# Which parts of g are turned by DMA is chosen per unit, and the table of leads is refitted, in a fused attention and mixture-of-experts kernel

## The chip, the cores and the metric

The kernel runs on one core of a Trainium2 chip, in one launch. Its time is the device time in microseconds, and a kernel's figure is the median of several runs. The core has a matrix engine (PE, with weight loads shown apart as PEld), a vector engine (DVE), an activation engine (ACT), a general engine (POOL) and a queue engine (SP) that issues most DMAs; a few are issued by ACT. Each engine works through its own instructions in the order in which they were written into the program, and waits at an instruction until what it needs is there.

## The reference

Three stages follow each other, all in float32, with 2304 = 4 x 576 tokens of 512 = 8 x 64 features. `tau` is 0.02, `E` is 8 experts with 4 slots each.

```python
scores = scale * np.matmul(q, k.transpose(0, 1, 3, 2))          # 4 x 8 heads, 576 x 576, 64 features a head
thresh = np.max(scores, axis=-1, keepdims=True) - tau
scores = np.where(scores >= thresh, scores, -1000000000.0)
attn = np.exp(scores - max); attn = attn / (sum + 1e-09)
x = concat of heads of np.matmul(attn, v)                       # 2304 x 512

g = np.maximum(x @ w_in, 0.0) ** 2                              # w_in 512 x 2048
x = g @ w_out                                                   # w_out 2048 x 512

logits = x @ phi                                                # phi 512 x 32
d = softmax of logits over the tokens
slot_input = d.T @ x                                            # 8 experts x 4 slots x 512
slot_out[e] = np.maximum(slot_input[e] @ w1[e], 0.0) @ w2[e]    # 512 x 1024 and 1024 x 512
out = softmax of logits over the slots @ slot_out
```

## The kernel before

The three stages are fused and overlap. **Attention** runs as 80 score tiles. For each, PE makes the scores (line L708 and its neighbours in the first tiles, in float32; L726 in the others, with float16 halves), DVE finds the maximum (L752), ACT takes the exponential (L764), DVE drops what is under the threshold (L768), ACT and POOL split the result into high and low halves (L787, L791), SP turns the halves by a DMA transpose (L798), and PE multiplies with v (L895, L900). DVE evacuates the result as rows of x.

**The FFN** works in nine units of 256 tokens, as soon as attention has delivered them. In each, x is split into float16 halves (L1214, L1219), and eight pairs of blocks follow, of 24 matmuls each (L1248; `f_a` and `f_b`), after which ACT applies relu (L1258) and the square (L1266). Their result, g, has tokens along its free axis: 16 blocks of 128 features by 256 tokens, in the tiles `gt`.

**What comes after a unit** is written by `post`, while the next unit's first pair runs. PE multiplies g with w_out phi to get logits (L1001, 16 instructions, of which the first 12 need the pairs 0 to 5 and the last 4 the pairs 6 and 7). ACT evacuates them into the tile l (L1079), PE adds up the partial sums (L1008) and transposes them (L1014), DVE updates the running maximum (L1026, L1028), ACT takes the exponential dT (L1032), and PE transposes that (L278 on dT). Then the weighted sum of g over the tokens is needed (L1166, into an accumulator, merged at L1176). For this, g must have its tokens along the partitions, so it is turned, in four parts `j` of a unit, each of two token blocks `t`. Either PE turns a part with 8 transposes of 128x128 (`f_turn`, printed as L278 on gt), and ACT evacuates it (`f_gk`, L1137); or the DMA turns it: ACT copies the part's two gt tiles side by side into a buffer of 16-bit halves (`f_part`, L1107, two instructions), SP issues one DMA transpose (`f_move`, L1112), and DVE puts the halves together again (`f_join`, L1147, four instructions). The buffers of this path are from the `raw64` pool, which the attention's loads use as well. The ninth unit's transposes are always on PE.

**The end.** The experts' weights (w1, w2) and w_out, in pieces of 0.5 or 1 MB, come by SP into buffers as these become free: some when attention's pools end, some (`w8`) as the last unit's L1248 have read w_in, some when the first tail matmuls (L1435) have read theirs. A hand-written tail (L1435 and later) turns the accumulated sums into slot inputs (with w_out), runs the experts (L1462, L1519, L1542, L1562) and writes the output (L1592, L1571).

**What sets the order.** Up to the tail, a planner (`Plan`) runs when the program is built. Each operation is added with an engine, a cost, what it depends on, the buffers that it takes and frees, and a key. At each step an engine takes, of the operations that are ready, that with the lowest key, and its instructions are written in this order. The key is a due time plus a number from the table `LEAD`, one for each kind of operation and each of five parts of the program:

```python
part = state.get("unit", 0) // 2 if abs(key) > FKEY / 2 else sum(key >= c for c in CUTS)
return plan.add(eng, cost, fn, deps, key + LEAD[kind][part], *args, ...)
```

So a changed table moves instructions on all engines, DMA issues among them, and no instruction's own work.

## Time and profile before

| | |
|---|---|
| median of 3 runs | 605.29 us (603.68 to 608.01) |
| the profiled execution | 604.63 us, its span 602.8 us |
| mean granted clock of PE | 0.993 |
| PE busy | 560.2 us (93%), its weight loads 387.7 (64%) |
| ACT busy | 464.8 us (77%) |
| DVE busy | 438.5 us (73%) |
| POOL busy | 290.8 us (48%) |

The profile is of one execution. Its span runs from the first to the last instruction, and the rest of its time lies around that. A busy share is a mean over stretches with different limits, so the rows that follow are mostly of single stretches, and of what an engine waited for there. In the chain that ended last each piece is what held up the next one, back from the last instruction. Matmuls are pipelined, so an instruction's mean duration is longer than its share of the busy time; the cost of one is the group's busy time divided by its count.

### The profile page before, as it was taken

How to read it: one execution, taken by the hardware profiler on the slowest of the kernel's cores; microseconds unless marked ns; L12 is line 12 of the kernel's file. 1: busy time of each engine (PE TensorE's matmuls, PEld its weight loads, DVE VectorE, ACT ScalarE, POOL GpSimd, SP SyncE). 2: the span in 40 equal slices, each digit the busy share in tenths (PEclk: the TensorE clock that was granted, in tenths of full speed). 3: DMA queues.
4: the chain of work that ended last, by engine and by line, in shares of the span. 5: the costliest groups of instructions: out<-in, count | busy, mean ns of one | idle time of the engine just before them, and what ended most of it. 6: DMA issues, size and time to landing. Idle time of an engine off the chain costs nothing.

```text
span 602.8 us, 14200 instructions
## 1 busy us (share of the span) xinstructions
PE 560.2 (93%) x5238; PEld 387.7 (64%) x5238; DVE 438.5 (73%) x1249; ACT 464.8 (77%) x880; POOL 290.8 (48%) x464
## 2 busy tenths in 40 slices
PE   1899998999999999999999999999999999999972
PEld 0556565656776787677677677767778777753331
DVE  3999999899969678888989999896951434232242
ACT  4899999898979897998998998998956776341122
POOL 1345875587857554875776486767620000010000
PEclk9999999899999999999999999999999999999998
DMA  8984574699956676659768767567629998999997
GB/s 266 368 277 132 177 263 147 196 217 211 227 106 135 129 149 154 119 134 171 159 101 167 145 124 115 109 125 132 121 40 301 232 318 201 335 369 360 407 323 261
DMA packets 171348, 120.97 MB, mean 201 GB/s; under 512 B 136592, under 2 KB 152720, under 8 KB 169360
## 3 DMA queue, kind: packets, MB, share of 16 engines
q1 hardware_dynamic: 170704, 117.98, 74.2%
q10 hardware_dynamic: 576, 2.10, 1.1%
q8 instruction: 41, 0.67, 0.5%
q14 instruction: 27, 0.22, 0.1%
HBM read 73.72 MB, written 8.91 MB: 137 GB/s over the span
## 4 chain that ended last, share of the span: by engine, by line
PE 70%; ACT 11%; DVE 9%; DMA 3%; issue 2%; POOL 2%; SPq 1%; DVEq 0%; ACTq 0%; POOLq 0%
PE mm L1248 30%; PE mm L278 8%; PE s L726 7%; PE po L895 5%; ACT raw L343 3%; PE mm L1166 3%; PE mm L1001 3%; ACT e L764 3%; DVE e L768 2%; PE mm L1462 2%; DVE u L752 2%; ACT pt L835 2%; PE mm L1519 2%; DMA w<-in_moe_w_dram 2%; DMA qt<-in_q_dram 1%
## 5 line engine op out<-in xcount | busy, mean ns | idle before, releaser
L1248 PEld LDWEIGHTS <-w 128*128 128x128 f16 x1728 | 166.1, 99 | 30.1 <-issue 11.5
L791 POOL TENSOR_TENSOR hl<-e,hl 128x288 f16<-128x288 f32 x192 | 148.5, 798 | 45.4 <-ACT hl L787 38.6
L1248 PE MATMUL mm<-xh,w 128*128 128x256 f16 x1152 | 149.7, 273 | 0.0
L768 DVE SCALAR_TENSOR_TENSOR e<-u,sm,e 128x576 f32<-128x576 f32 x144 | 122.5, 869 | 14.8 <-ACT e L764 11.1
L764 ACT ACTIVATE e<-u,sm 128x576 f32<-128x576 f32 x144 | 109.1, 772 | 9.4 <-DVE u L752 5.7
L758 POOL TENSOR_SCALAR sm<-sm,tau_p 128x1 f32<-128x1 f32 x144 | 79.3, 556 | 66.9 <-DVE u L752 55.9
L1248 PE MATMUL mm<-xl,w 128*128 128x256 f16 x576 | 86.4, 273 | 0.0
L752 DVE TENSOR_SCALAR_CACHE_REDUCE u<-s,raw 128x576 f32<-128x576 f32 x90 | 71.3, 808 | 7.7 <-PE s L726 7.3
L1258 ACT ACTIVATE gt<-mm,scl 128x512 f32<-128x512 f32 x72 | 49.2, 683 | 34.2 <-PE mm L1248 34.1
L787 ACT ACTIVATE hl<-e 128x576 f16<-128x576 f32 x96 | 63.9, 677 | 2.6 <-DVE e L768 2.1
L1412 POOL MEMSET cv<- 128x512 f32 x4 | 1.9, 527 | 97.8 <-PE mm L1166 97.8
L752 DVE TENSOR_SCALAR_CACHE_REDUCE u<-s,nscale 128x576 f32<-128x576 f32 x54 | 42.8, 809 | 5.7 <-PE s L713 5.4
L343 ACT ACTIVATE raw<-raw 128x512 f16<-128x512 bf16 x32 | 43.1, 1367 | 4.2 <-DMA raw<-in_moe_w_in_dram 4.2
L1266 ACT ACTIVATE gt<-gt 128x512 f32<-128x512 f32 x72 | 45.0, 625 | 1.0
L726 PEld LDWEIGHTS <-qt 128*128 128x128 f16 (+3 forms) x400 | 22.1, 99 | 25.5 <-issue 17.4
L855 POOL TENSOR_SCALAR sm<-sm 128x4 f32<-128x4 f32 (+1 forms) x48 | 20.4, 424 | 35.4 <-DVE e L768 32.3
L895 PE MATMUL po<-pt,vh 128*64 128x256 f16 x576 | 36.0, 275 | 0.0
L726 PE MATMUL s<-kt,qt 128*128 128x512 f16 (+1 forms) x200 | 32.9, 289 | 1.8 <-DVE u L752 1.6
L895 PEld LDWEIGHTS <-vh 128*64 128x64 f16 x576 | 29.6, 110 | 5.6 <-issue 5.4
L835 ACT ACTIVATE pt<-mm 128x512 f32<-128x512 f32 x48 | 28.6, 610 | 5.3 <-PE mm L278 5.1
L1137 ACT ACTIVATE gk<-mm 128x512 f32<-128x512 f32 x50 | 27.1, 595 | 5.8 <-PE mm L278 5.7
L278 PE MATMUL mm<-ident_r,e 128*128 128x128 f32 x192 | 30.0, 286 | 1.3 <-DVE e L768 1.0
(211 smaller groups left out, 987.0 us busy)
## 6 DMA issues: line engine op xcount, KB each, us to landing
w<-in_moe_w_dram SPq DMA_DIRECT2D x15, 1024.0 KB, 9.7
w<-in_moe_w_dram SPq DMA_DIRECT2D x26, 512.0 KB, 8.0
raw<-in_moe_w_in_dram SPq DMA_DIRECT2D x16, 511.8 KB, 7.0
raw<-in_moe_w_out_dram SPq DMA_DIRECT2D x16, 511.8 KB, 4.0
raw<-in_v_dram SPq DMA_DIRECT2D x20, 256.0 KB, 4.0
w_out<-cv SPq DMA_DIRECT2D x16, 256.0 KB, 3.5
w<-w_out SPq DMA_DIRECT2D x8, 512.0 KB, 7.6
kt<-in_k_dram SPq DMA_DIRECT2D x10, 320.0 KB, 4.1
```

What stands on the lines that cost most here:

```text
L278: nc.tensor.transpose(out_, in_, ident[:n, :n])
L343: nc.scalar.activation(x[:, :, 3].bitcast(F16), x[:, :, 2].bitcast(BF16), AF.Copy)
L726: nc.tensor.matmul(o0, d["qh"][r, a, q0], kk, start=full, stop=not full)
L752: nc.vector.tensor_scalar(u, o["s"][:, s0:s0 + S], d.get("nscale", nscale), None, ALU.mult, ALU.min, accum_out=gd["sm"][:, c:c + 1])
L758: nc.gpsimd.tensor_scalar(sm[:, 4 + c:5 + c], sm[:, c:c + 1], tau_p, None, ALU.add)
L764: nc.scalar.activation(e, o["u", a], AF.Exp, scale=-1.0, bias=gd["sm"][:, c:c + 1])
L768: nc.vector.scalar_tensor_tensor(e, o["u", a], sm[:, 4 + c:5 + c], e, ALU.is_le, ALU.mult, accum_out=sm[:, 8 + c:9 + c])
L787: nc.scalar.activation(o["hl"][:, a * S:(a + 1) * S], o["e"][:, a * S:(a + 1) * S], AF.Copy)
L791: nc.gpsimd.tensor_tensor(o["hl"][:, 2 * S:][:, i], o["e"][:, i], o["hl"][:, i], ALU.subtract)
L895: nc.tensor.matmul(po[64 * a:64 * a + 64, :n_], d["vh"][:, y, c0:c0 + D], gd["pt"][:, :, c + 5 * a + m, :], start=i == 0 and m == 0, stop= ...
L1248: nc.tensor.matmul(o["h"][:, i * NU:(i + 1) * NU], a, c, start=n_ == 0, stop=n_ == len(terms) - 1)
L1258: nc.scalar.activation(g, o["h"], AF.Relu, scale=down)
```

## The change

The tuple `DTU`, the units all of whose parts are turned by DMA (6 and 7, that is eight parts), becomes a table from a unit to its parts: part 0 of unit 4, parts 0 and 1 of unit 5, parts 0 to 2 of the units 6 and 7, nine parts in all. `post` takes the parts in place of a yes or no. All numbers of `LEAD` are other ones (some 84 kinds of operations, of five numbers each; the first kind is shown).

```diff
-    LEAD = {'av': (-596.3, -409.2, -386.7, -356.8, -339.1),
...
+    LEAD = {'av': (-187.2, -271.7, -238.7, -182.9, 37.2),
...
-    DTU = (6, 7)
+    DTU = {4: (0,), 5: (0, 1), 6: (0, 1, 2), 7: (0, 1, 2)}
...
-            for j in range(NG) if by_halves else ():
+            for j in by_halves:
...
-                    if by_halves:
+                    if j in by_halves:
...
-            pending = lambda u=u, d=d, n=n: post(u, d, n == 0, n == len(units) - 1, n in DTU)
+            pending = lambda u=u, d=d, n=n: post(u, d, n == 0, n == len(units) - 1, DTU.get(n, ()))
```

In instructions: PE has 216 instead of 224 transposes of g (L278), ACT has 18 instead of 16 copies (L1107) and two evacuations (L1137) fewer, DVE has 36 instead of 32 copies (L1147), SP nine instead of eight transposes (L1112). All else is as often there as before, in another order. In the middle of the program attention's tiles come earlier in PE's order: ahead of the 41st score tile stand 264 instead of 384 L1248, ahead of the last ones nearly the same number. At the start of SP's order five instead of four loads of w_in (L331) stand ahead of the first loads of k and q. Three places follow.

**The end of the last unit, on PE.** Before, twelve of the unit's L1001 stand among its last matmuls (w_126 is a block of w_in; xh and xl are the halves of x):

```order
L1248 LDWEIGHTS w_126
L1248 MATMUL mm<-xl,w_126 128x256
L1001 MATMUL mm<-gt,wphi 32x256 x12
L1248 LDWEIGHTS w_126
L1248 MATMUL mm<-xh,w_126 128x256
```

and the last four stand behind the last matmul, ahead of the transposes:

```order
L1248 LDWEIGHTS w_126
L1248 MATMUL mm<-xl,w_126 128x256
L1001 MATMUL mm<-gt,wphi 32x256 x4
L278 MATMUL mm<-ident_r,gt 128x128 x8
L1008 MATMUL mm<-l_79,stack_f 32x256
L278 MATMUL mm<-ident_r,gt 128x128 x20
```

After the change all sixteen stand there:

```order
L1248 LDWEIGHTS w_126
L1248 MATMUL mm<-xl,w_126 128x256
L1001 MATMUL mm<-gt,wphi 32x256 x16
L278 MATMUL mm<-ident_r,gt 128x128 x8
L1008 MATMUL mm<-l_79,stack_f 32x256
L278 MATMUL mm<-ident_r,gt 128x128 x20
L278 MATMUL mm<-ident_r,dT 128x32 x2
```

So the twelve L1001 have moved behind the last L1248.

**Behind the second unit's logits, on PE.** Before, the last four L1001 stand ahead of products of attention (L887) and of a score tile, which begins with L726:

```order
L278 MATMUL mm<-ident_r,e 128x128 x4
L278 MATMUL po<-ident_r,e 64x128
L278 MATMUL mm<-ident_r,rp 128x128
L1001 MATMUL mm<-gt,wphi 32x256 x4
L887 MATMUL po<-pt,raw 64x64 x8
L887 MATMUL po<-pt,vbd_129 64x64 x2
L726 LDWEIGHTS qt
L726 MATMUL s<-kt,qt 128x512
```

and after the whole tile and 16 transposes of g, L1008 and L1014 follow:

```order
L726 LDWEIGHTS qt
L726 MATMUL s<-raw_2050,qt 128x512
L278 MATMUL mm<-ident_r,gt 128x128 x16
L1008 MATMUL mm<-l_79,stack_f 32x256
L1014 MATMUL mm<-stack_f,l_79 128x32 x2
L1248 LDWEIGHTS w_120
```

After the change the tile stands ahead of the L1001, and this is all that stands between:

```order
L726 LDWEIGHTS qt
L726 MATMUL s<-raw_2494,qt 128x512
L278 MATMUL mm<-ident_r,gt 128x128 x12
L1001 MATMUL mm<-gt,wphi 32x256 x4
L278 MATMUL mm<-ident_r,gt 128x128 x4
L1008 MATMUL mm<-l_79,stack_f 32x256
L1014 MATMUL mm<-stack_f,l_79 128x32 x2
L1248 LDWEIGHTS w_120
L1248 MATMUL mm<-xh,w_120 128x256
```

Twelve transposes and the tile have moved ahead of the last four L1001; four transposes are left between them and L1008.

**The end of attention, on SP.** Before, the last probability transposes (pt) are followed by weight loads, each of 1 MB, and the transposes of g of the units 6 and 7 (raw) in groups:

```order
L798 DMA_TRANSPOSE pt<-hl 128x18x128 x4
L541 DMA raw<-in_v_dram 128x2x256
L798 DMA_TRANSPOSE pt<-hl 128x18x128 x4
L1321 DMA w<-in_moe_w_dram 128x2048 x3
L1112 DMA_TRANSPOSE raw_7176<-raw_7067 128x16x128
L1112 DMA_TRANSPOSE raw_7239<-raw_7208 128x16x128
L1321 DMA w<-in_moe_w_dram 128x2048
L1112 DMA_TRANSPOSE raw_7303<-raw_7269 128x16x128
L1112 DMA_TRANSPOSE raw_7362<-raw_7336 128x16x128
L1321 DMA w<-in_moe_w_dram 128x2048 x4
L1112 DMA_TRANSPOSE raw_7573<-raw_7464 128x16x128
```

After the change transposes of g stand among those of attention, and single ones among the weight loads:

```order
L798 DMA_TRANSPOSE pt<-hl 128x18x128 x3
L1112 DMA_TRANSPOSE raw_6427<-raw_6379 128x16x128
L798 DMA_TRANSPOSE pt<-hl 128x18x128 x3
L1112 DMA_TRANSPOSE raw_6763<-raw_6639 128x16x128
L798 DMA_TRANSPOSE pt<-hl 128x18x128 x2
L1112 DMA_TRANSPOSE raw_7096<-raw_7057 128x16x128
L1321 DMA w<-in_moe_w_dram 128x2048 x2
L1112 DMA_TRANSPOSE raw_7214<-raw_7188 128x16x128
L1112 DMA_TRANSPOSE raw_7289<-raw_7259 128x16x128
L1321 DMA w<-in_moe_w_dram 128x2048 x4
L1112 DMA_TRANSPOSE raw_7487<-raw_7422 128x16x128
L1321 DMA w<-in_moe_w_dram 128x2048
```

So four transposes of g, one of them further up in the order, have moved ahead of the first weight loads.

## Rows read from the trace of the kernel before

**Rows 1.** Windows: stretch and length, then busy us (instructions) by engine, clock, DMA.

```profile
0.00:20.00 20.00, 6.96 (x36) 4.15 (x36) 10.01 (x28) 9.86 (x12) 2.64 (x10) 1.00 0.90 299
20.00:100.00 80.00, 73.59 (x534) 46.49 (x535) 77.94 (x223) 79.14 (x145) 48.79 (x78) 1.00 0.69 229
130.00:228.00 98.00, 96.56 (x991) 72.24 (x991) 81.10 (x230) 86.61 (x174) 65.97 (x101) 1.00 0.78 165
230.00:450.00 220.00, 217.59 (x2220) 159.34 (x2218) 190.44 (x550) 193.84 (x388) 149.44 (x240) 1.00 0.66 129
545.00:587.00 42.00, 39.18 (x350) 15.66 (x350) 12.80 (x36) 7.51 (x15) 0.00 (x0) 1.00 1.00 370
```

**Rows 2.** Waits of PE, 130 to 542: line, released by, us in total, times, longest.

```profile
PE mm L1001 <- ACT gt L1266: 0.9, 1, 0.9
PE mm L278 <- ACT dT L1032: 0.4, 1, 0.4
PE mm L1014 <- ACT dT L1032: 0.4, 1, 0.4
```

**Rows 3.** Chain that ended last, 524 to 546: start us, us, what.

```profile
525.09 1.43 PE mm L1001 x24
...
526.52 4.05 PE mm L1248 x36
...
531.32 0.64 ACT gt L1266
...
541.18 3.76 PE mm L1435 x32
```

**Rows 4.** Chain that ended last, 570 to 603.

```profile
576.76 9.53 DMA w<-in_moe_w_dram
```

**Rows 5.** Waits of SP's queue, 440 to 603.

```profile
SPq L1112 <- ACT gt L1258: 20.0, 3, 11.8
...
SPq L1321 <- PE mm L1248: 15.0, 4, 5.1
```

**Rows 6.** Lines by form: out<-in, shapes, count | busy us, mean ns | idle before.

```profile
L1248 PE MATMUL mm<-xh,w 128*128 128x256 f16 x1152 | 149.7, 273 | 0.0
...
L1248 PE MATMUL mm<-xl,w 128*128 128x256 f16 x576 | 86.4, 273 | 0.0
...
L1258 ACT ACTIVATE gt<-mm,scl 128x512 f32<-128x512 f32 x72 | 49.2, 683 | 34.2 <-PE mm L1248 34.1
...
L1266 ACT ACTIVATE gt<-gt 128x512 f32<-128x512 f32 x72 | 45.0, 625 | 1.0
...
L343 ACT ACTIVATE raw<-raw 128x512 f16<-128x512 bf16 x32 | 43.1, 1367 | 4.2 <-DMA raw<-in_moe_w_in_dram 4.2
...
L278 PE MATMUL mm<-ident_r,gt 128*128 128x128 f32 x224 | 30.2, 278 | 0.1
...
L1107 ACT ACTIVATE raw<-gt 128x1024 uint16<-128x1024 uint16 x16 | 16.8, 1053 | 0.4
...
L1147 DVE COPY gk<-raw 128x512 uint16<-128x512 uint16 x32 | 11.9, 446 | 12.3 <-DMA raw<-raw 12.2
...
L1079 ACT ACTIVATE l<-mm 128x256 f32<-128x256 f32 x9 | 3.4, 380 | 3.8 <-PE mm L1001 3.8
```

**Rows 7.** Line L798: duration ns min/median/max, first and last start; DMA landing us.

```profile
L798 SPq DMA_TRANSPOSE pt<-hl x48: 2455/2712/4457, 124.3 to 441.3; - x48
...
DMA to landing us min/median/max: 4.6/4.8/7.2
```

**Rows 8.** Timeline of PE, 449 to 458: start us, us, line, operation.

```profile
451.01 1.50 PE L895 MATMUL po<-pt,vh 128*64 128x256 f16 x24
```

**Rows 9.** Windows of two stretches of 5 us.

```profile
500.00:505.00 5.00, 5.00 (x60) 3.51 (x59) 2.38 (x6) 4.47 (x7) 0.00 (x0) 1.00 0.66 120
560.00:565.00 5.00, 5.00 (x48) 2.02 (x44) 2.24 (x16) 0.60 (x1) 0.00 (x0) 1.00 1.01 415
```

**Rows 10.** Timeline of PE, 226 to 231.

```profile
228.31 0.41 PE L726 MATMUL s<-kt,qt 128*128 128x512 f16 x2
```

More of the change, by code (lines that the diff above doesn't have):

```diff
@@ new lines, in tile_kernel @@
+    LEAD = {'av': (-187.2, -271.7, -238.7, -182.9, 37.2), 'bound': (-120.4, 49.3, -257.6, -97.6, -119.3), 'c_evac': (-64.7, 2.3, -128.1, -64.7, -64.7), 'c_load': (-24.4, -19, -19.1, -16.9, -16.9), 'c_low': (179.1, 284.8, 324.2, 256.7, 256.7), 'c_out': (-275.7, -534, -267.5, -275.7, -275.7), 'c_prod': (452.7, 369.4, 377.6, 452.7, 452.7), 'c_scale': (281, 345.5, 353.4, 230.4, 230.4), 'c_shift': (-79.8, -63.1, -9, -28.9, -28.9), 'c_store': (-54.1, 168.6, 5.4, -54.1, -54.1), 'c_strip': (-124.2, -97.2, -62, -124.2, -124.2), 'c_total': (199.1, 337.5, 163.6, 199.1, 199.1), 'c_turn': (78.3, -14.4, 31.5, 78.3, 78.3), 'dturn': (0.2, 0.2, 4.7, 1, 31.4), 'eps': (289.2, 168.3, 43.9, 315.2, 289.6), 'evac': (-336.9, -168.3, -188.3, -182.3, -180.9), 'expo': (-11.8, -8.9, 10.8, 16.6, 146.4), 'f_a': (12.7, 53.1, 177.4, 179.9, 245), 'f_acc': (7.7, -153.5, 139.3, -43.7, -17.3), 'f_alpha': (-429.2, -178.3, -177.1, -60.8, -37.9), 'f_b': (-32.2, -84.5, -276.1, -291.8, -14.2), 'f_ce': (50.7, 201, 42.5, 49.9, 172.7), 'f_cmax': (-162.3, 3.2, -143.5, -331.5, -181.8), 'f_csum': (426, 268.4, 43.6, 5.5, 127.9), 'f_dk': (-133.5, 22, -249.9, -82.1, -83.6), 'f_gk': (-40.9, 79.4, 62.1, -9.3, -102.3), 'f_join': (-6.7, -6.7, -2.5, -5.9, -6.7), 'f_l4': (-367.8, -299.2, -145, -124.1, -89.7), 'f_max': (-125.8, -144.8, -77.5, -157.4, -195.2), 'f_merge': (-8.8, 194.5, 146.5, 5.3, 261.4), 'f_move': (-83.3, -83.3, -100, -24.5, -83.3), 'f_p12': (-138.7, -271.6, -154.6, -109, -132), 'f_p1k': (-18.8, -213.8, -77.8, 14.3, -11.6), 'f_p3': (-733, -321.4, -206, -373.1, -440), 'f_part': (206.1, 206.1, 200.5, 275.4, 206.1), 'f_pl': (229.6, 332.1, 262.7, 269.5, 306.5), 'f_pm': (-201.3, -85.5, -276, -214.9, -136.5), 'f_relu': (62.1, -241.7, -68.9, -106.8, -187.1), 'f_rs': (-126.5, -126.5, -126.5, -126.5, -78.4), 'f_sq': (-16.9, -6.5, -142.8, -77.9, -68.1), 'f_total': (-37.6, 152.8, -48.2, 68.7, -46.6), 'f_turn': (-249, -45.7, -0.9, -11.4, -19.9), 'high': (-106.1, -106.1, -119.3, -69.1, -26.4), 'keep': (-114.5, -61.7, -50, -55, 23.5), 'low': (-44.8, -44.8, -161.7, -82.8, -61.3), 'lphi': (-45, -45.7, -45, -45, -45), 'lraw': (-5.1, 19.9, 14, -5.6, -22.5), 'lrem': (-5, -8.1, 154, 96.4, -8.1), 'p_evac': (-75.2, -108.9, -204.2, -37.7, 55.4), 'q_hi': (-132.4, -132.4, -52.2, -44.7, -68.1), 'q_lo': (176.9, 176.9, 333.6, 234.7, 313.5), 'q_move': (0.2, 0.2, 4.1, 1.8, 66.1), 'q_scale': (-77.3, -77.3, 27.4, -86.8, -363.5), 'q_sq': (424.2, 424.2, 234.7, 244.6, 369.6), 'q_sum': (-357.8, -357.8, -116.5, -491.4, -298.5), 'r_evac': (-10.6, -0.1, -47.5, -30.3, -12.1), 'r_turn': (-191.3, -63, -57.4, -59.8, -56.2), 'recip': (-126.8, -97, -81, -55, -62.2), 's': (-165.9, -48.1, -26.3, 2.5, 103.5), 'spread': (8.4, 61.2, 88.2, 129.6, 146.5), 'top': (-38.9, 31.7, 34, 43.6, 64.9), 'turn': (-28.4, -13.2, 0.5, -2.1, 26.2), 'v_abs': (-179.2, -5.9, -61.1, 19.4, 125), 'v_hi': (-152.8, -152.8, -122.8, -247, -210.3), 'v_lo': (-78.3, -78.3, -28, -40.2, -113.6), 'v_scale': (-285.6, -126.6, -241.4, -160.6, -356.2), 'v_sum': (-185.7, -145.3, -124.9, -191.3, -137), 'w_diag': (123.9, 101.2, 150.9, 150.9, 150.9), 'w_diff': (-93.1, -138.4, -130.2, -130.2, -130.2), 'w_gram': (71.9, 126.2, 136.8, 136.8, 136.8), 'w_hi': (72.3, 15.9, 21.7, 21.7, 21.7), 'w_id': (-291.9, -110.7, -176.1, -176.1, -176.1), 'w_lo': (-319.5, -331.1, -296.5, -296.5, -296.5), 'w_load': (-3.5, -187.4, -187.4, -187.4, -187.4), 'w_pre': (-58.7, -100, -100, -100, -100), 'w_rest': (308.8, -71, 70.3, 70.3, 70.3), 'w_round': (278.9, 334.5, 292.8, 292.8, 292.8), 'w_scale': (59.3, 90.8, 60.2, 60.2, 60.2), 'w_sum': (-110.5, -71, -68.7, -68.7, -68.7), 'w_times': (57.9, 168.4, -50.5, -50.5, -50.5), 'w_wide': (203.1, 203.1, 203.1, 203.1, 274.2), 'x_scale': (105.6, 57.9, 57.9, -29.2, -125.9), 'xhi': (63.7, 183.9, 245, 246.5, 296.6), 'xlo': (-7.3, 70.4, 78.5, 91.9, 202.5)}
```

1 line of the change is left out of this document (removed).

## The prediction

> **What bounds the kernel now.** I read the busy shares by stretch first, then what the PE waits for, then the chain that ended last, then the prices by line. Up to 130 us ACT is the bound: in the stretch from 20 to 100 it is busy 79.14 of 80 us and DVE 77.94, PE 73.59 [rows 1]. From about 130 us, where the first FFN matmuls run, PE is the bound: 96.56 of the 98 us from 130 to 228 and 217.59 of the 220 us from 230 to 450 [rows 1]. The reader should see that ACT and DVE are at 83 to 88% in these two stretches, close behind. The waits of PE confirm it: single waits of 0.9, 0.4 and 0.4 us [rows 2] and little else in 400 us. The chain shows the one clear gap, at the end of the last unit: L1248 ends at 526.52 + 4.05 = 530.57 us, relu and square follow on ACT until 531.32 + 0.64 = 531.96, and only then do the last four L1001 start [rows 3]. At the very end the weight stream is the bound: from 545 to 587 us the DMA share is 1.00, and PE stands from 576.76 for 9.53 us until the last weights land [rows 1, 4]. So a saved microsecond counts if PE is spared it between 130 and 541 us, provided that the stream moves along; most of its loads wait for space that PE frees (L1321 behind L1248, 15.0 us in four waits [rows 5]), so I let it move along.
>
> The profiled execution took 604.63 us with a span of 602.8, the median of the runs is 605.29. All terms change the span; I add their sum to the median.
>
> **The change, part by part.**
>
> *Transposes on PE.* Nine of the parts of g go by DMA instead of eight, so 8 of 224 transposes fall away, at 30.2 / 224 = 0.135 us [rows 6]: **-1.1 us**, on the bound engine. With them go two evacuations on ACT.
>
> *The copies that the DMA path needs.* Before the end of attention 3 parts are added: 6 ACT copies L1107 of 1.053 us = 6.3 us and 12 DVE copies L1147 of 0.446 us = 5.4 us [rows 6]. In units 6 and 7 two parts fall away again. ACT has 26 us of idle time between 230 and 450 us and DVE 30 [rows 1]: I cost them at nothing. Were that cover gone, ACT would hold PE up by up to 6.3 us.
>
> *The queue.* On SP four transposes of g (L1112; the three new ones and the first of unit 6) stand among the attention's probability transposes (L798), which wait behind them. The last L798 is issued at 441.3 us, takes 4.8 us to land in the median [rows 7], and its user L895 starts at 451.01 [rows 8]: 4.9 us of slack. A transpose holds the queue for 2.7 us [rows 7]. Nothing, then; at worst four times the part of a longer wait beyond the slack, some 3 us. The weight loads now stand between single L1112. Before, SP stood 20.0 us in three waits of L1112 for ACT [rows 5], with weight loads behind it, and the stream was still gated later by PE. Nothing again.
>
> *A page's rule on this path.* The row first: from 500 to 505 us, while only transposes moved, the DMA engines were busy at 0.66 and moved 120 GB/s, against 415 GB/s from 560 to 565 us with plain weight loads [rows 9]. The Trainium skill (Advanced Engine Details and Errata, X-Bar Transpose (TRN2)) says that transpose DMAs are as fast as regular ones. By that, a part of 0.5 MB would cost the stream 0.5 MB at 415 GB/s, an estimate of 1.3 us; by the row it costs 0.5 MB at 120 GB/s = 4.4 us, though the transposes there may be few rather than slow. The sum holds neither, since the stream waits for PE; the first rival uses the price by the row.
>
> *End of the last unit.* The order of the changed kernel puts the twelve L1001 that stood inside the last matmuls behind them. They take 1.43 us on PE [rows 3], and the relu and square for which the last four wait take 1.39 us from 530.57 us to 531.96. So the wait is filled: at most -1.4, at least -0.9 by the wait that the list of waits shows [rows 2]. I take **-1.2 us**.
>
> *The dT waits.* L1014 and L278 waited 0.4 us each on the exponent dT of L1032 [rows 2]. In the changed order of units 5 and 6 transposes and at least 24 L1248 stand ahead of them; in unit 7 twelve L1248 of 0.137 us do, with perhaps 0.2 us left to wait. **-0.6 us.**
>
> *The cover of l.* Between the last L1001 of a unit and L1008, which needs ACT's evacuation L1079 (0.38 us [rows 6]), units 0 and 1 now have only 4 transposes, 0.54 us; before, a whole score tile stood there. If L1079 stands behind one 0.68 us instruction of ACT [rows 6], PE waits 0.38 + 0.68 - 0.54 = 0.5 us, in two units, and units 2 to 5 have more cover. Bounds 0 and 1.5; **+0.6 us**.
>
> *The start.* One more load of w_in of 0.5 MB stands ahead of q and k. At the 299 GB/s of the first 20 us [rows 1] that is +1.7 us; but the expansions L343 of 1.367 us [rows 6] can go into the first 20 us, of which ACT was busy for only 9.86 [rows 1], two more of them by the order: -2.7. Bounds +1.7 and -2.7, middle **-0.5 us**.
>
> *Denser attention in the middle.* In PE's order 264 L1248 stand ahead of the 41st score tile, and 384 did; the tile starts at 228.31 us [rows 10]. 120 matmuls of (149.7 + 86.4) / 1728 = 0.137 us [rows 6] are 16.4 us, so PE can be there at 211.9, 81.9 us after 130 instead of 98.3. What ACT and DVE have to do ahead of the tile changes little, save that five pairs of relu and square fall away: 5 x (0.683 + 0.625) = 6.5 us [rows 6]. ACT did 86.61 us from 130 to 228 [rows 1]; 80.1 are left, 98% of 81.9. DVE's 81.10 are 99%. Not all of it is for tiles this early, since both worked ahead. Lower bound 0, since in 20 to 100 us ACT did run at 99%. Upper bound by ACT's pace when PE binds, 86.61 / 98 = 0.884: 80.1 / 0.884 = 90.6, which is 8.7 us late; and by DVE's, 81.10 / 98 = 0.83, 98 us, 16 us late. The stretch is nearest to that of 20 to 100 us, where attention alone ran and DVE kept 97%: 81.10 / 0.974 = 83.3, or 1.4 late, less what was ahead. I take **+1.0 us**.
>
> Sum: -1.1 - 1.2 - 0.6 - 0.5 + 0.6 + 1.0 = **-1.8 us**, from 605.3 to **603.5 us**.
>
> **Rivals.**
>
> *The stream at the end is what shrinks (faster).* Two of the transposes of units 6 and 7 no longer lie among the first weight loads: 2 x 4.4 us by [rows 9]. If the stream is thereby ahead all the way, the 9.53 us for which PE stands on it at the end [rows 4] shrink by 8.8: 603.5 - 8.8 = 594.7. For it: DMA share 1.00 from 545 us. Against: loads wait for PE's L1248 before that [rows 5]. In half of it, some 599.
>
> *Attention's bound moves to ACT and DVE (slower).* The dense stretch above, with ACT and DVE at the pace that they kept before: 8.7 to 16 us late, 12.5 in the middle, in place of 1.0: 603.5 + 11.5 = 615.0. For it: the shares of 98 and 99%, where before neither had to keep more than its 83 to 88%. Against: from 20 to 100 us both kept 97 to 99% [rows 1]. It makes the kernel slower by 1% once the tile is over 8.9 us late, so at an ACT pace under 0.88.
>
> *Nothing comes of it.* PE's busy time may hide slack: a matmul record may last long while the array could take the next one, so that fewer transposes and shorter waits are made up elsewhere: 605.3. For it: the weight loads PEld are busy 159.34 us where PE is 217.59 [rows 1]. Against: PE leaves 2.4 of 220 us idle [rows 1], and L1248 costs the same 0.137 us wherever it runs. The Trainium skill (Perfetto Trace Analysis, Identifying the Most-Contended Engine) holds matmul busy time to be a poor measure of the headroom and asks for weight-load busy time instead; by that, PE has room left, and this rival holds.
>
> **How the numbers follow.** My forecast, with its terms within their bounds, has 0.52 and nothing at all 0.11; the stream has 0.22 and the denser attention 0.15. About 1%, 6 us, is what a measurement of this kernel can tell from no change, so the borders are 599.2 and 611.3. Of the stream's 0.22, 0.18 ends below 599.2, and 0.04 comes to that from a weak form of it together with the small terms at their low ends, which sum to about -6: faster 0.22. Of the denser attention 0.11 ends above 611.3: slower 0.11. The same 0.67. The range has to leave no more than 0.2 outside: below 596.0 lies 0.08, the strongest form of the stream, and above 609.5 lies 0.12, the denser attention with 7 us or more. That is 596.0 to 609.5.
>
> **What would show it.** PE's list of waits without L1001 on L1266 and without dT; L1435 starting some 2 us before 541.18 [rows 3]; the 41st score tile near 212 us instead of 228.31, with no more than 1 to 2 us of PE waits for DVE or ACT before it; the last weights landing about 2 us before 586.3. Wrong I would be if PE shows waits of several us on DVE or ACT between 130 and 230 us (second rival), if L895 waits for its transposed tile (the queue), or if the last load lands early while L1435 does not start earlier (first rival).

## The result and the profile after

The change makes the kernel slower: 613.55 us (median of 4 runs, 612.0 to 614.3) against 604.48 us for the kernel before on the same chip. The ratio is 1.0138, with a 95% interval of 1.0114 to 1.0161. Forecast were 603.5 us and a range from 596.0 to 609.5. The profiled execution took 612.0 us with a span of 610.2; before it was 604.63 and 602.8, so the two profiles differ by 7.4 us. The changed kernel's profile is of its fastest run, so the last 1.7 us between the medians are not in it.

Windows after, moved along with the work that stood in the windows of [rows 1]. The columns are as there (PE, PEld, DVE, ACT, POOL, clock, DMA share, GB/s):

```profile
0.00:20.00 20.00, 8.02 (x30) 3.88 (x30) 10.98 (x32) 12.36 (x14) 3.63 (x11) 1.00 0.91 301
20.00:100.00 80.00, 70.87 (x481) 43.71 (x480) 70.71 (x199) 75.14 (x134) 40.60 (x74) 1.00 0.63 209
137.00:235.00 98.00, 94.92 (x958) 69.39 (x958) 89.60 (x238) 87.81 (x176) 69.43 (x110) 1.00 0.81 162
237.00:457.00 220.00, 216.42 (x2214) 158.51 (x2215) 191.78 (x538) 194.01 (x383) 145.57 (x233) 1.00 0.69 134
552.00:594.00 42.00, 39.35 (x352) 16.22 (x350) 12.81 (x36) 7.54 (x15) 0.00 (x0) 1.00 1.01 371
```

From the first FFN matmul on PE is nearly as full as before; from 20 to 100 us nothing is: ACT fell from 79.14 to 75.14 and DVE from 77.94 to 70.71, in a stretch in which both had been close to full. In the first 20 us both had done more than before (ACT 2.50 us, DVE 0.97). So at 100 us ACT is 1.5 us of work behind the kernel before, and DVE 6.3. PE's timeline has the first FFN matmuls of the kernel before, then of the one after:

```profile
130.02 1.04 PE L1248 MATMUL mm<-xh,w 128*128 128x256 f16 x8
```

```profile
137.34 1.05 PE L1248 MATMUL mm<-xh,w 128*128 128x256 f16 x8
```

They come 7.3 us late, which is the whole difference of the two profiles. The chain of the kernel after shows it carried to the end, around the last unit and at the last weights:

```profile
530.97 7.09 PE mm L1248 x65
538.07 2.07 PE mm L1001 x31
...
548.68 3.76 PE mm L1435 x32
```

```profile
584.01 9.64 DMA w<-in_moe_w_dram
```

L1435 starts 7.50 us after the 541.18 of [rows 3], and the last weights land at 593.65 instead of 586.29 [rows 4], 7.36 us late. From the first L1248 to the first L1435 it is 411.2 us before and 411.3 after. The window over that stretch, first of before and then of after, says what is behind this equality:

```profile
130.00:541.20 411.20, 405.64 (x4051) 300.84 (x4050) 302.92 (x870) 336.76 (x649) 218.56 (x346) 1.00 0.75 172
```

```profile
137.30:548.70 411.40, 404.48 (x4044) 299.92 (x4039) 312.66 (x869) 337.44 (x650) 218.20 (x348) 1.00 0.76 172
```

PE is busy 1.16 us less, and idle 6.92 instead of 5.56 us. Its waits there, as in [rows 2], begin in the kernel before with two lines that [rows 2] does not show, and then come those of after:

```profile
PE s L726 <- DVE u L752: 1.6, 4, 0.6
PE s L708 <- DVE u L752: 1.2, 1, 1.2
```

```profile
PE s L726 <- DVE u L752: 1.8, 4, 0.9
PE s L708 <- DVE u L752: 1.2, 2, 0.9
PE mm L278 <- ACT gk L1137: 1.0, 1, 1.0
PE mm L278 <- DVE cv L351: 0.9, 2, 0.5
PE po L640 <- ACT qt L634: 0.8, 2, 0.6
PE mm L1014 <- ACT dT L1032: 0.3, 1, 0.3
...
PE mm L278 <- ACT dT L1032: 0.2, 1, 0.2
```

The wait of L1001 is gone, those on dT fell from 0.8 to 0.5 us, and new waits for ACT and DVE have come in their place, on L1137, L351 and L634, of 2.7 us together. The two on L752 were there before.

### The profile page after: what moved, and what is told of

It reads as the page before. It is cut to its first block, busy times and chain, and to the rows that moved or that the text cites. A ratio compares the mean times of both kernels' runs of the same rounds, so it can differ in the third digit from the quotient of the medians.

```text
span 610.2 us, 14167 instructions
## 1 busy us (share of the span) xinstructions
PE 562.4 (92%) x5230; PEld 387.8 (64%) x5230; DVE 449.9 (74%) x1253; ACT 466.8 (76%) x880; POOL 283.0 (46%) x464
## 4 chain that ended last, share of the span: by engine, by line
PE 64%; DVE 13%; ACT 10%; DMA 2%; issue 2%; POOL 1%; SPq 0%; DVEq 0%; ACTq 0%; POOLq 0%
PE mm L1248 27%; PE mm L278 7%; PE s L726 6%; PE po L895 4%; DVE u L752 4%; DVE e L768 3%; ACT e L764 3%; PE po L887 2%; PE mm L1166 2%; PE mm L1001 2%; PE mm L1462 2%; ACT raw L343 2%; PE mm L1519 2%; DMA w<-in_moe_w_dram 2%; ACT pt L835 1%
## 5 line engine op out<-in xcount | busy, mean ns | idle before, releaser
L1248 PEld LDWEIGHTS <-w 128*128 128x128 f16 x1728 | 165.9, 98 | 28.9 <-issue 10.2
L791 POOL TENSOR_TENSOR hl<-e,hl 128x288 f16<-128x288 f32 x192 | 153.2, 817 | 46.7 <-ACT hl L787 28.1
L1248 PE MATMUL mm<-xh,w 128*128 128x256 f16 x1152 | 149.7, 273 | 0.1
L768 DVE SCALAR_TENSOR_TENSOR e<-u,sm,e 128x576 f32<-128x576 f32 x144 | 126.3, 889 | 13.2 <-ACT e L764 12.0
L758 POOL TENSOR_SCALAR sm<-sm,tau_p 128x1 f32<-128x1 f32 x144 | 72.3, 502 | 71.1 <-DVE u L752 67.0
L1248 PE MATMUL mm<-xl,w 128*128 128x256 f16 x576 | 86.4, 273 | 0.0
L752 DVE TENSOR_SCALAR_CACHE_REDUCE u<-s,raw 128x576 f32<-128x576 f32 x90 | 71.3, 806 | 2.2 <-PE s L726 1.6
L343 ACT ACTIVATE raw<-raw 128x512 f16<-128x512 bf16 x32 | 43.0, 1369 | 6.7 <-DMA raw<-in_moe_w_in_dram 6.7
L752 DVE TENSOR_SCALAR_CACHE_REDUCE u<-s,nscale 128x576 f32<-128x576 f32 x54 | 42.5, 809 | 1.5 <-PE s L713 1.3
L726 PEld LDWEIGHTS <-qt 128*128 128x128 f16 (+3 forms) x400 | 22.0, 99 | 27.2 <-issue 19.3
L855 POOL TENSOR_SCALAR sm<-sm 128x4 f32<-128x4 f32 (+1 forms) x48 | 18.7, 389 | 40.5 <-DVE e L768 36.7
L895 PE MATMUL po<-pt,vh 128*64 128x256 f16 x576 | 36.0, 275 | 0.0
L726 PE MATMUL s<-kt,qt 128*128 128x512 f16 (+1 forms) x200 | 32.9, 289 | 1.9 <-DVE u L752 1.8
L895 PEld LDWEIGHTS <-vh 128*64 128x64 f16 x576 | 29.6, 110 | 7.7 <-issue 6.0
L278 PE MATMUL mm<-ident_r,e 128*128 128x128 f32 x192 | 30.1, 287 | 3.1 <-DVE e L768 2.6
L726 PE MATMUL s<-raw,qt 128*128 128x64 f16 (+1 forms) x200 | 31.2, 293 | 0.0
```

Source lines behind the costliest of these rows:

```text
L278: nc.tensor.transpose(out_, in_, ident[:n, :n])
L343: nc.scalar.activation(x[:, :, 3].bitcast(F16), x[:, :, 2].bitcast(BF16), AF.Copy)
L726: nc.tensor.matmul(o0, d["qh"][r, a, q0], kk, start=full, stop=not full)
L752: nc.vector.tensor_scalar(u, o["s"][:, s0:s0 + S], d.get("nscale", nscale), None, ALU.mult, ALU.min, accum_out=gd["sm"][:, c:c + 1])
L758: nc.gpsimd.tensor_scalar(sm[:, 4 + c:5 + c], sm[:, c:c + 1], tau_p, None, ALU.add)
L768: nc.vector.scalar_tensor_tensor(e, o["u", a], sm[:, 4 + c:5 + c], e, ALU.is_le, ALU.mult, accum_out=sm[:, 8 + c:9 + c])
```

## The experiments

The question is thus why the first L1248 is late. Up to it, but for a handful of operations, only the order of instructions differs. Each row is one kernel; "first L1248" and "L1435" are starts in its own profile, in us.

| kernel | median us | ratio to before, 95% | first L1248 | L1435 |
|---|---|---|---|---|
| before | 604.48 | | 130.0 | 541.2 |
| after | 613.55 | 1.0138 (1.0114 to 1.0161) | 137.3 | 548.7 |
| e1_after_warm | 611.37 | 1.0096 (1.0064 to 1.0128) | 138.4 | 549.6 |
| e2_old_attention_leads | 640.47 | 1.0592 (1.0559 to 1.0626) | 127.9 | 576.1 |
| e3_new_attention_leads | 623.59 | 1.0309 (1.0257 to 1.0361) | 139.8 | 562.6 |
| e4_new_leads_old_parts | 617.33 | 1.0218 (1.0166 to 1.0271) | 138.2 | 551.4 |
| e5_after_gram_behind | 613.88 | 1.0145 (1.0122 to 1.0167) | 137.1 | 548.5 |
| e6_before_gram_ahead | 607.08 | 1.0041 (1.0023 to 1.0059) | 132.2 | 543.5 |
| e7_after_hot | 612.84 | 1.0125 (1.0103 to 1.0148) | 138.9 | 550.0 |
| e8_before_hot | 605.68 | 1.0020 (0.9996 to 1.0043) | 130.5 | 541.8 |
| e9_after_before_start | 606.50 | 1.0028 (1.0008 to 1.0048) | 131.1 | 543.3 |
| e10_before_after_start | 612.54 | 1.0140 (1.0107 to 1.0172) | 138.3 | 549.0 |
| e11_before_after_start5 | 606.92 | 1.0050 (1.0027 to 1.0073) | 131.7 | 542.8 |
| e12_before_after_start17 | 609.25 | 1.0089 (1.0065 to 1.0114) | 134.8 | 545.9 |
| e13_after_order_from_tile4 | 613.25 | 1.0139 (1.0110 to 1.0168) | 140.3 | 550.4 |
| e14_after_order_from_tile16 | 613.92 | 1.0157 (1.0129 to 1.0186) | 139.4 | 549.0 |
| e15_before_one_l1001_block | 604.38 | 0.9984 (0.9965 to 1.0003) | 130.5 | 540.7 |
| e16_after_more_dve_late | 623.40 | 1.0298 (1.0264 to 1.0331) | 140.6 | 557.4 |
| e17_after_more_act_late | 615.26 | 1.0161 (1.0122 to 1.0201) | 141.9 | 553.9 |
| e18_after_more_act_early | 620.04 | 1.0262 (1.0216 to 1.0309) | 147.4 | 558.3 |

### The first theory: a slow PE at the start

In the kernel before PE does nothing until the first q and k are there. In the changed order the first 16 Gram products of w_in (L422), in four groups with gaps, stand ahead of the first score tile. Timeline of PE, first before, then after:

```profile
13.56 2.08 PE L713 MATMUL s<-kt,qt 64*128 64x512 f32 x4
...
17.78 1.13 PE L713 MATMUL s<-kt,qt 64*128 64x512 f32 x4
```

```profile
9.66 0.60 PE L422 MATMUL mm<-gt 128*128 128x128 bf16 x4 [1.08 <-DVE gt L351]
...
24.59 2.08 PE L713 MATMUL s<-kt,qt 64*128 64x512 f32 x4
...
29.79 1.13 PE L713 MATMUL s<-kt,qt 64*128 64x512 f32 x4
```

The same four L713 take 2.08 us at the lower of the clock's two levels and 1.13 at the upper. Before they are fast from 17.78 us on, after only from 29.79. So the theory was that the early, thin L422 keep PE slow for 12 us longer, against the rival that the order of everything up to 130 us is what costs. Two kernels warm PE up with transposes into a tile that nobody reads, the first with 12 ahead of everything, the other between the L422 also:

```diff
+            warm = mm_tile()
+            for _ in range(12):
+                transpose(warm[:, 0:128], ident)
             plan.run(att)
```

> The changed kernel with 12 transposes of the identity put ahead of everything on PE (into a tile that nobody reads), in the 8 us in which PE has nothing to do; no other instruction moves. Clock theory: the changed kernel lost its time at the start, since PE stayed at the lower clock until about 28 us (its second score tile's four L713 took 2.08 us, the kernel before's 1.13). Then the second tile's L713 take about 1.1 us here, the first L1248 starts 3 to 5 us earlier than 137.3, and the kernel takes 608 to 611 us where the changed one takes 613.5. Rival (the new order of w_in's conversion and attention on ACT and DVE is what costs): L713 is faster, but the first L1248 starts within 1.5 us of 137.3, and the time stays at 612 to 614.

> The changed kernel with transposes of the identity into an unread tile wherever PE pauses in the first 18 us: 12 ahead of everything, 4, 3 and 3 between the groups of L422, 5 behind the first score tile. The order of all else as in the changed kernel. Clock theory: even the first tile's L713 take 1.1 us, PE is never at the lower clock after 13 us; first L1248 at 132 to 134.5 us, kernel 608 to 611 us. Rival: the first tiles are earlier, but the first L1248 is at 136 or later, 612 to 614.

Neither made a kernel that was warm at the right time. In e1 L713 took 1.13 us from 24.17 us on, but the first L1248 came at 138.4, and its interval touches that of the change itself. In e7, with PE busy nearly without a gap from 7.92 us on, the L713 of 24.36 us still took 2.08 us. Both say little for or against. Moving the L422 themselves does: e5 is the changed kernel with the first 16 of them behind the first score tile, e6 is the mirror, the kernel before with them ahead of it, and no other engine's order differs. In e5 the edit runs the Gram products (`gram`) and `diag`, which reads them, at the end of the tile's function; in e6 it runs the first tile's function at the end of `gram`:

```diff
-                gg = add("w_gram", "PE", 1.1, gram, deps, k, ["mm"])
+                gg = add("w_gram", "PE", 1.1, gram if f4 else lambda: (gram(), state["first"]()), deps, k, ["mm"])
-                S_ = add("s", "PE", (0.6 if mixed else 0.9) if p >= QF else 1.4, s_mm, d["ready"], k, ["s"])
+                S_ = add("s", "PE", (0.6 if mixed else 0.9) if p >= QF else 1.4, lambda: s_mm() if "first" in state else state.update(first=s_mm), d["ready"], k, ["s"])
```

> The changed kernel with one thing moved on PE: the sixteen L422 that it has ahead of the first score tile stand right behind that tile, as in the kernel before; the order on DVE, ACT, POOL and SP is that of the changed kernel. Clock theory: PE now works without a pause from the first score tile through the L422, is at the upper clock by the second tile (four L713 in 1.1 us in place of 2.08), the first L1248 starts at 133 to 135 us in place of 137.3, and the kernel takes 609.5 to 611.5 us in place of 613.5. Rival (the order of conversion and attention on ACT and DVE is what costs): the first L1248 at 136.5 or later, 612.5 to 614.

> The mirror: the kernel before with its first sixteen L422 moved ahead of the first score tile on PE, where the changed kernel has them; all other engines as before. Clock theory: the L422 run in four groups with gaps, as their blocks of w_in come in, PE pauses behind the first tile, and the second tile still runs at the lower clock (2.08 us for its four L713); first L1248 at 132.5 to 135 us in place of 130.0, kernel 607 to 609.5 us. Rival: 604 to 606, first L1248 before 131.5.

e6 is slower by 2.5 us (0.23 to 0.59%), and its profile has the first L1248 2.2 us later. Early Gram products do cost something. But e5 is no faster than the changed kernel (613.88 against 613.55): DVE waits 3.86 us for the moved L422 at L425, and the first L1248 comes at 137.1 in place of 137.3. Nor did it make PE fast by the second tile, as was expected: the L713 there still take 1.99 us, and those of the third tile, at 25.62 us, are the first to take 1.13. The last of this group, the kernel before with 30 transposes ahead of everything, asks what a warm start is worth at all:

> The kernel before with 30 transposes of the identity into an unread tile ahead of its first score tile, where PE stands idle until 12.86 us. Clock theory: the first tile's L713 take 1.1 us instead of 2.08 and its L708 0.46 instead of 0.77, ACT starts its first exponential about 1.3 us earlier, and with ACT as the bound up to 130 us the first L1248 starts at 128 to 129.5 us: 603 to 604 us, 1 to 2 less than before. Rival (the start is bound by the loads of w_in and by ACT's conversion anyway): no change, 604.3.

Its first L713 takes 1.13 us, at 13.13 us, and the kernel isn't faster (0.9996 to 1.0043), though from 12 to 24 us its granted clock is only 0.65 to 0.79, so that it isn't warm throughout. So neither kernel shows that a PE slow by 2 us in the first tiles sets the time, and e6, which has both the early Gram products and the slow tiles, loses 2.5 us. The theory falls as the explanation of the 9 us.

### Parts of the table

The leads of the attention and of the FFN can't be taken apart. e2 is the changed kernel with the old leads of all kinds that are not the FFN's, e3 the kernel before with the new ones of these kinds, e4 the changed kernel with the old parts:

```diff
-    DTU = {4: (0,), 5: (0, 1), 6: (0, 1, 2), 7: (0, 1, 2)}
+    DTU = {6: (0, 1, 2, 3), 7: (0, 1, 2, 3)}
```

> The changed kernel with the leads of all operations outside the FFN (attention, conversion of the weights, loads) as before; the FFN's leads and the nine parts are the new ones. The order of the first 500 PE instructions is that of the kernel before. If the start is what costs: the first L1248 at 130 to 131 us, and a time of 602 to 606 us, like the kernel before. If the FFN's new order or the new choice of parts costs: 610 or more.

> The other half: leads of all operations outside the FFN are the new ones, the FFN's leads and the eight parts of the units 6 and 7 as before. Start theory: first L1248 at 137 us as in the changed kernel, 611 to 615 us. Rival (parts or FFN leads cost): 603 to 607.

> The changed kernel with all new leads, but the parts of g as before (all four of the units 6 and 7). What the parts alone are worth at the new leads. My step: eight transposes more on PE, 1.1 us slower than the changed kernel, 613 to 616. If the three DMA parts during attention cost something: 1 to 4 us faster than the changed kernel.

All three are slower than both kernels. The numbers of one table were fitted together, so a half of each gives orders that nobody fitted, and the middle of the program grows (448 us from the first L1248 to L1435 in e2, 423 in e3, 413 in e4, against 411). That e2, with the old leads of the attention, has its first L1248 at 127.9 and e3 at 139.8 points to the start; no more is to be had from these. What the choice of parts alone is worth stays open too, since in e4 the order differs with it: it costs 3.8 us to go back, with leads fitted for the new parts.

### The order up to the first L1248, whole and in pieces

To move an order and nothing else, the planner gets a list of operations, and an engine may take only the one whose turn it is; behind the list it goes on by its keys. e9 is the changed kernel with the order of before, word for word on all five engines, up to the first L1248, and e10 the mirror.

```diff
-                    ok = [o for o in self.cand[e] if o.ready <= self.now + self.wait and self.fits(o)]
+                    ok = [o for o in self.cand[e] if o.ready <= self.now + self.wait and self.fits(o) and (not TURN[e] or TURN[e][0] == o.n)]
```

> The changed kernel with the order of all engines up to the first L1248 taken word for word from the kernel before (the same operations but for a handful), and from there on the changed kernel's own order and parts. If the whole loss lies in the order of the start: first L1248 at 130 to 131 us, from there 411 us to L1435 as in the changed kernel, 603 to 606 us in all. If the later order or the parts cost: 609 or more.

> The mirror: the kernel before with the changed kernel's order of all engines up to the first L1248, its own order and parts after it. Start theory: first L1248 at 136 to 138 us, 610.5 to 614 us. Rival: within 2 us of the kernel before.

The time goes with the start. PE's timeline of e9, then of e10:

```profile
131.07 1.04 PE L1248 MATMUL mm<-xh,w 128*128 128x256 f16 x8
```

```profile
138.30 1.05 PE L1248 MATMUL mm<-xh,w 128*128 128x256 f16 x8
```

The old start takes the changed kernel from 1.0138 to 1.0028 (1.0008 to 1.0048), the new start takes the kernel before to 1.0140. So the order of the first 130 us costs some 1.1% (e9) to 1.4% (e10), and all the rest of the change between nothing (e10) and 0.3% (e9). The 1.4% hold some 3 us of a slower clock, which fell in e10 and not in the changed kernel (last section). Then the pieces: the kernel before with the new order up to the 5th tile (some 30 us) or the 17th (some 90 us), and with the new order only from the 4th (some 22 us) or the 16th tile (some 85 us) to the first L1248.

> The kernel before with the changed kernel's order only up to the fifth score tile (58 rows of PE, 44 of DVE, 36 of ACT, about the first 30 us); then its own. It holds the early L422 and the low clock, and the first conversions of w_in ahead of tiles. Lower clock as most of the loss: first L1248 at 134 to 137 us, 608.5 to 613. If the order between 30 and 130 us costs as much: 132 to 134, 606.5 to 608.5, that is no more than what the L422 alone cost (2.5 us).

> As the last, but up to the seventeenth score tile (235 rows of PE, about the first 90 us). If the loss is made in the first 30 us: as the last one within 1 us. If it comes bit by bit: first L1248 1.5 to 3 us later than in the last one, 609 to 612 us.

> The kernel before, its own order for the first three score tiles (46 rows of PE, to about 22 us), then the changed kernel's order of all engines up to the first L1248, then its own again. The start is thereby at the upper clock and without the early L422, and what is left is the changed order of conversion and attention between 22 and 130 us. If that order costs by itself: first L1248 at 134 to 136.5 us, 609 to 611.5 us (the 8 us of the whole start less the 2.4 of its first 30 us). If the loss needs the low clock and the late tiles of the first 30 us: under 132.5 us, 604 to 606.5.

> The same with the kernel before's order up to the fifteenth score tile (230 rows of PE, to about 85 us), and the changed order only from there to the first L1248. If the losses of the stretches add up: first L1248 at 132.5 to 134 us, 607 to 608.5 us. Rival: no later than 131, 604 to 606.

Each against the kernel before in its own series, the new order costs 2.4 us up to the 5th tile, 4.8 up to the 17th, and from the 16th tile alone 8.8, about as much as all of it. The pieces don't add up: the new order from 85 us on arrives at 137 to 140 us whatever preceded it, so that what its first 85 us cost is hidden behind it. In e10, e13 and e14 some 3 us of this are a lower clock just ahead of the first L1248 (last section), so the sizes of the pieces are rough. That a better start came to nothing in e5 fits this, but e5 too lost clock, with PE granted 0.50 from 126 to 128 us.

What is different from 85 us on shows on SP, which works through its loads in order. Waits of SP's queue from 85 to 130 us, for before, e12, after and e14:

```profile
SPq L331 <- DVE cv L351: 6.7, 3, 3.6
```

```profile
SPq L331 <- DVE cv L351: 15.6, 6, 4.5
```

```profile
SPq L331 <- DVE cv L351: 26.8, 6, 13.5
```

```profile
SPq L331 <- DVE cv L351: 25.0, 6, 15.8
```

L331 loads a block of w_out into a buffer that DVE's L351 frees by joining an earlier block. In the changed order one of these loads stands at the head of the queue for 13.5 us, and behind it are loads of v, k and q (L541, L550). The longest wait of the kernel before there is 7.2 us, of an L541 for PE's L887. SP's timeline of after:

```profile
94.94 0.93 SPq L393 DMA_DIRECT2D w_out<-cv  x2
109.39 0.33 SPq L331 DMA_DIRECT2D raw<-in_moe_w_out_dram  x1
109.82 1.63 SPq L541 DMA_DIRECT2D raw<-in_v_dram  x1
...
112.05 0.38 SPq L550 DMA_DIRECT2D kt<-in_k_dram  x1
112.48 0.42 SPq L550 DMA_DIRECT2D qt<-in_q_dram  x1
```

The windows from 100 us on, first of before and then of after, show the loads' pause and what follows:

```profile
100.00:110.00 10.00, 8.71 (x62) 5.54 (x59) 9.01 (x21) 7.86 (x16) 8.32 (x13) 0.83 0.35 102
110.00:120.00 10.00, 9.36 (x88) 5.99 (x90) 8.83 (x23) 10.00 (x19) 3.98 (x7) 1.00 0.69 216
120.00:130.00 10.00, 8.76 (x75) 4.98 (x74) 9.70 (x33) 9.93 (x21) 8.30 (x13) 1.00 0.80 189
```

```profile
100.00:110.00 10.00, 9.67 (x89) 6.29 (x83) 9.07 (x26) 7.76 (x16) 6.17 (x12) 1.00 0.01 3
110.00:120.00 10.00, 8.32 (x68) 5.20 (x70) 9.60 (x28) 7.01 (x15) 2.44 (x6) 1.00 0.87 305
120.00:130.00 10.00, 7.19 (x74) 4.75 (x70) 9.88 (x27) 10.00 (x21) 5.56 (x7) 1.00 0.87 272
```

From 100 to 110 us 3 GB/s are moved in place of 102; then loads of w_out and of the attention arrive together. DVE, which must expand the one and scan the other, does 28.55 of 30 us, 1.0 more than before, and by that makes up little of the 6.3 us by which it was behind. ACT, the bound of [rows 1], runs out of work (7.01 us from 110 to 120), by its waits mostly for PE's L278. All twelve kernels that have the new order in this stretch have the wait of L331, at 13.1 to 15.8 us (after, e1, e3, e4, e5, e7, e10, e13, e14, e16, e17, e18); in the eight others (before, e2, e6, e8, e9, e11, e12, e15) it is 4.5 us at most. Yet e12 is late by 4.8 us without it. And the chain of the changed kernel from 60 us to the first L1248 has no DMA in it: it runs through ACT, DVE and PE by turns, and the only wait of the three for a load from 100 to 130 us is one of 0.7 us, ACT's L573 for v. So the wait marks where DVE's L351 has come to stand late; that the late loads cost time themselves isn't shown. A run that takes the wait away alone wasn't made, and which of the leads puts the L351 so late stays open.

### Which engine sets the pace

If DVE binds from 100 us on and ACT before that, extra work on each must cost in its stretch and not elsewhere. e16 does L351 twice in the last 8 blocks of w_out (4.9 us more on DVE in all), e17 L343 twice in 4 of these (5.0 us more on ACT), and e18 L343 twice in 4 blocks of 62 to 82 us (5.0 us on ACT). The diff is of e16:

```diff
-                nc.vector.scalar_tensor_tensor(
+                for _ in range(2 if n in range(24, 32) else 1): nc.vector.scalar_tensor_tensor(
```

> The changed kernel with the shift and join L351 done twice (same result) for the last eight blocks of w_out: 8 x 0.61 = 4.9 us more on DVE between about 100 and 137 us, the order as in the changed kernel. If DVE sets the pace of that stretch there (it is busy 96 to 99% of 110 to 130 us, ACT 70 and 100%): the first L1248 starts 3.5 to 5 us later, at 141 to 142.5, and the kernel takes 616.5 to 619 us. If it doesn't: under 1.5 us.

> The changed kernel with the expansion L343 done twice for four of the last eight blocks of w_out: 4 x 1.24 = 5.0 us more on ACT in the same stretch, where ACT stands idle for 7 us. If DVE sets the pace: the first L1248 at most 2 us later, 613 to 616 us. If ACT does: 4 to 5 us later, as in the run with more work on DVE.

> The changed kernel with L343 done twice for four blocks that it expands between 62 and 82 us: 5.0 us more on ACT where ACT is busy 100% and DVE 83 to 90%. If ACT sets the pace of that stretch: the tile whose L708 starts at 97.7 us comes 3.5 to 5 us later, 101 to 102.5. If DVE or PE does: under 1.5 us later.

By the ratios to the kernel before, against the changed kernel's 1.0138, e16 costs 1.6% more, e18 1.2% and e17 0.2%, which is within its interval. The early stretch has a clear answer: in e18 the tile whose L708 started at 97.70 us starts at 104.14, 6.4 us late, so from 60 to 90 us ACT is on the path. (That is more than the 5.0 us that were added; PE's mean clock fell to 0.90 there as well.) The window of e18 from 60 to 90 us has ACT at 29.09 of 30 us, and DVE far below:

```profile
60.00:90.00 30.00, 23.92 (x141) 13.56 (x141) 20.82 (x56) 29.09 (x46) 15.60 (x29) 0.90 0.35 116
```

For the late stretch the two runs don't decide between the engines. By the times DVE looks to be on the path and ACT not. By the sign that the expectations name, the first L1248, it is the other way about: it starts 3.3 us late in e16, under what was expected of a DVE that binds, and 4.6 us late in e17, what was expected of an ACT that binds. Three things blur both. Only two of e16's eight doubled L351 come ahead of its first L1248 (28 of these instructions stand there, 26 in the changed kernel), so that most of its extra work, and 5.5 of the us that it loses, fall behind it: from there to L1435 it takes 416.8 us in place of 411.3. PE's clock fell in both ahead of the first L1248, and not in the changed kernel (last section). And e17's profiled execution, at 618.15 us, is its slowest, 2.9 us above its median. So which engine sets the pace from 100 us on stays open; for DVE speaks that it is the fullest there, and that it comes to 100 us with the most work left.

### The end of the last unit by itself

e15 is the kernel before with the last unit's twelve L1001 behind its last matmul, nothing else:

```diff
-            a0 = add("f_pl", "PE", 1.53, lambda: pl(0, MC // NG - 1), d["sq"][:-2] + (conv if first else []), pk(), ["mm"])
+            a0 = add("f_pl", "PE", 1.53, lambda: pl(0, 0 if last else MC // NG - 1), d["sq"][:-2] + (conv if first else []), pk(), ["mm"])
```

> The kernel before with one thing of the change done alone: the last unit's twelve L1001 stand behind its last L1248 with the other four, all else in its old order. My term for this was -1.2 us (bounds -0.9 and -1.4). L1435 then starts at 539.8 to 540.3 us in place of 541.2, and the time is 0.9 to 1.4 us below that of the kernel before. Rival: the weight stream holds the end, and nothing moves.

Its chain has no gap there any more:

```profile
524.73 5.35 PE mm L1248 x48
530.07 2.07 PE mm L1001 x31
...
540.69 3.76 PE mm L1435 x32
```

From the first L1248 to L1435 it takes 410.2 us, 1.0 less than before. The whole (0.9965 to 1.0003) allows for that, and for nothing. No kernel here is faster than the kernel before by more than its interval.

## Why the prediction was wrong

**The step that failed is "The start", taken at -0.5 us with bounds of +1.7 and -2.7; it measured +7.3 us** (first L1248 at 137.34 in place of 130.02), or 1.1 to 1.4% of the time by e9 and e10. It looked at one more load ahead of q and k, and at ACT's idle time in the first 20 us. There it was near: the first L708, which waits for q, starts at 13.17 in place of 12.86 us, so the load cost 0.3 of the 1.7 us, and ACT did 2.5 us more by 20 us, close to the 2.7. The loss came behind that, where no term stood. The gap was in front of me: I wrote that ACT bounds the kernel up to 130 us, at 79.14 of 80 us [rows 1], and that a changed table moves instructions on all engines, and then followed the order on all engines only behind 130 us. An engine at 99% in a stretch is that full in this order. For a new order it is the best case, and no floor: from 20 to 100 us ACT lost 4.0 us of busy time and DVE 7.2, while the work ahead of the first L1248 hardly changed (ACT is busy 116.81 and 118.14 us up to it, DVE 115.50 and 117.21). And I named ACT alone as the bound: what ACT lost was in part done earlier, and DVE, at 77.94 of 80 us in [rows 1], was left with the larger arrears, 6.3 us at 100 us. The order of the start as a whole is shown to be the cause, by e9 and e10; by which waits within it DVE and ACT lost their time is not. The bounds were wrong because both came from the first 20 us. And of SP's queue I followed the transposes at the end of attention, not the loads of w_out, where the longest new wait is.

**Transposes, -1.1.** Right as to PE's busy time, 1.16 us less between the first L1248 and L1435. But that a saved microsecond of PE counts there didn't hold: the stretch is no shorter, since new waits took the place.

**The copies, nothing.** Right as to ACT's copies: no wait of PE is on them. The price of one L1147 rose from 0.446 to 0.484 us [rows 6], off the path:

```profile
L1107 ACT ACTIVATE raw<-gt 128x1024 uint16<-128x1024 uint16 x18 | 19.0, 1056 | 0.4
...
L1147 DVE COPY gk<-raw 128x512 uint16<-128x512 uint16 x36 | 14.8, 484 | 0.0
```

**The queue, nothing.** Right for the place that was looked at: PE's list of waits has no L895.

**End of the last unit, -1.2 (bounds -0.9 and -1.4).** Right: no L1001 in the waits, none in the chain, and -1.0 in e15, by itself.

**The dT waits, -0.6.** Half: 0.8 became 0.5 us.

**The cover of l, +0.6.** No L1008 waits. But behind the second unit's last L1001, in the gap that was priced, PE waits 1.0 us at the four transposes for ACT's L1137. ACT was late there as feared, with another of its instructions, and not in both units.

**Denser attention, +1.0.** The 41st score tile starts at 220.85 us, 83.5 behind the first L1248, where 81.9 was the earliest: 1.6 late, near the forecast. But the 81.9 rests on 0.137 us for an L1248, the busy times of the xh and xl groups added, and these overlap at their ends. The chain has 36 in 4.05 us [rows 3], or 0.11 each; so the cost of one is less than a group's busy time divided by its count. By the chain's price 120 are 13.5 us, the earliest is 84.8, and the tile isn't late at all. The agreement is luck. New waits of PE for DVE and ACT between its first L1248 and L1435 come to what the rest saves, so that 411.2 us stay 411.3. Without the start the steps were to sum to -1.3 us; measured is +0.2.

**The rivals.** The second one's time (615.0) is close to the measured 613.55, but not its mechanism: it put ACT and DVE as the bound between 130 and 228 us, where PE stayed the bound. They lost their time ahead of 130 us. The first rival did not come: SP's L1112 stands 26.1 us in three waits for ACT's L1107 (16.1 in two before), and the last load's piece is 9.64 us long, against 9.53. "Nothing comes of it", for which a page's rule spoke (the Trainium skill, Perfetto Trace Analysis, Identifying the Most-Contended Engine), isn't borne out either way by the total. Its reason, slack under the busy matmuls, isn't seen: where PE was 98% busy, a shift of the first L1248 by 7.3 us moved L1435 by 7.5.

## What to carry to other kernels

When a table of priorities is refitted, compare the orders in every stretch in which some engine is full, beginning with the first, and give "same work, other order" a loss there of its own, with the idle time that the other engines would add as its bound; a stretch at 99% can hardly gain. Count for each of the full engines, and not for the fullest alone, how much of its work is done by a given time. Follow each in-order queue for loads that wait for a buffer, and then ask the chain whether anything needed what stands behind them. To find where an order loses, splice the one into the other up to a point, and again from that point on: the two need not add up, and the later piece can hide all that the earlier one cost or saved. When extra work is put on an engine to see whether it binds, count how much of it comes ahead of the point that is timed.
